# One SBUF port for GpSimd and VectorE in a kernel's scheduler, the float64 shift on ScalarE or VectorE, and longer TensorE fillers

## The chip, the cores and the metric

The kernel runs on one core of one Trainium2 chip. The metric is device time in microseconds (us), the median of several runs of the same program. The engines are named as in the profile: PE is TensorE, PEld its weight loads, DVE is VectorE, ACT is ScalarE, POOL is GpSimd, SP issues the DMAs.

## The reference

Attention (local over a band of seven positions, plus pooled over groups of four) feeds two feed-forward mixtures, all in float32; the weights arrive as float64.

```python
x = attention(q, k, v).transpose(0, 2, 1, 3).reshape(2304, 512)   # 4 batches, 8 heads, 576 x 64
h = x @ w_in                       # 512 -> 2048, float64 weights
x = (h * np.cos(h)) @ w_out        # 2048 -> 512
xn = x / rms * rms_g
g, val = xn @ w_gate, xn @ w_val   # 512 -> 1536
return (silu(g) * val @ w_out2).astype(np.float32)
```

## The kernel before

The program is straight-line code whose order a list scheduler (`Order`, a planner that runs while the program is built) decides. Every stage is a Python generator; before it emits instructions it yields the engine and an assumed duration, or a list of alternatives (engine, duration, release time, activation table, bias). `start` picks the alternative that ends first, bias included; `run` advances the clock of that engine and lets the step of the earliest start and due time go first. So the durations and biases in the `yield` lines set the order of each engine's queue and which engine takes a movable step; on the chip each engine executes its queue in that order, whatever the real durations.

The stages, in the order in which they fill the time:

- Batch 0 of the attention: pooled queries and keys (`sum4`, `pq_ev`, `pooled`), pooled values on POOL (L499 to L506), and five band blocks (`block`): transposes (`btr`, L641), scores (`bs`, L684), softmax on DVE and ACT with a final scaling by the reciprocal sum (L706, on POOL or DVE), a transpose (`bat`, L720) and the product with the values (`bav`, L745). `pooled` scales its exponentials by the reciprocal sum at L555 (POOL or DVE). The sum of both parts is split into a high and a low fp32r half (L768 on ACT, L770 on POOL) and is one tile X.
- Weights. `w_conv` turns a float64 word pair into a high and a low fp32r matrix: a right shift by 29 of the low word (L311, DVE), a `Prelu` that rescales the high word (L315, ACT), a shift-and-or (L317, DVE), a copy to the high half (L319, ACT) and a subtraction for the low half (L322, POOL or DVE; the bias CVB of 9 keeps it on POOL). There are 32 such pieces for the first mixture. `w2_conv` (L1295 to L1299) does the first three steps for 36 pieces of the second mixture. A raw piece occupies one of five places until its last step, and the next weight DMA on SP waits for a place.
- First mixture: 72 units. A unit is `h` on PE (L1004), scaled to integers on ACT (L1022), reduced on DVE (L1024), a sine on ACT (L1027), a product on DVE (L1029), then split into halves `gh` on ACT (L1038) and `gl` on POOL or DVE (L1040, bias GLB), and `y` on PE (L1070). Batches 1 to 3 of the attention run beside it, and exponentials and sines load different activation tables on ACT.
- Second mixture: norms, `gvp` (L1493) and `o` (L1746).

`keep_warm` (L246) puts float32 matmuls into pauses of PE that the planner foresees before its time FT = 90, if a PSUM bank is free: the number is FR = 0.8 of the pause, divided by 0.22.

```python
    n = int((t1 - max(t0, 2.5)) * FR / 0.22)
    have = [x for x in S_.pools["bank"] if x[0] <= t0]
    if t0 > FT or n < 1 or not have:
        return
```

## Time and profile before

| | |
|---|---|
| runs | 984.79 us median (983.96 to 986.35, 3 runs) |
| the profiled execution | 986.51 us, its span 984.7 us |
| PE busy | 954.6 us (97%) |
| DVE, ACT, POOL busy | 724.0, 542.8, 268.5 us |
| mean granted PE clock | 0.994 |

PE is busy nearly all the time, so the view to start from is busy time by stage, then what ended each idle stretch of PE, then the lines of the other engines in the stages where PE is idle. A busy PE can still hold matmuls that do no useful work (the fillers), and in a half-clock stretch it is busy for twice as long.

### The profile page before, as it was taken

The page shows a single profiled execution, that of the slowest core. Times are in us where ns is not written, and L with a number is a line of the kernel's source. Part 1 is how long each engine was busy: PE and PEld are TensorE (multiplying, and loading weights), DVE is VectorE, ACT ScalarE, POOL GpSimd, SP SyncE. Part 2 cuts the span into 40 slices and gives each one's busy share as a digit, 9 for nine tenths or more (in the row PEclk, how much of TensorE's full clock was granted, in tenths as well). Part 3 has the DMA queues.
Part 4 walks back from the last instruction along what each step waited for, and adds up shares of the span by engine and source line. Part 5 has one row for each costly group of instructions (what it writes and reads, how often), then busy time and mean ns, then how long its engine had stood idle before and what let it go on. Part 6 is the DMA issues. An engine that isn't in the chain of part 4 may idle for free.

```text
span 984.7 us, 19115 instructions
## 1 busy us (share of the span) xinstructions
PE 954.6 (97%) x7102; PEld 881.4 (90%) x7102; DVE 724.0 (74%) x1460; ACT 542.8 (55%) x1090; POOL 268.5 (27%) x325
## 2 busy tenths in 40 slices
...
GB/s 245 211 234 252 179 116 118 140 204 185 201 220 153 173 168 137 167 153 165 124 129 65 107 43 49 49 105 93 75 81 70 57 146 131 137 169 137 143 119 76
DMA packets 160333, 136.07 MB, mean 138 GB/s; under 512 B 72176, under 2 KB 133744, under 8 KB 160240
## 3 DMA queue, kind: packets, MB, share of 16 engines
...
q8 instruction: 56, 0.92, 0.4%
q14 instruction: 37, 0.30, 0.1%
HBM read 98.64 MB, written 36.18 MB: 137 GB/s over the span
## 4 chain that ended last, share of the span: by engine, by line
PE 83%; POOL 4%; DVE 3%; SPq 3%; issue 3%; DMA 2%; ACT 2%; DVEq 0%; POOLq 0%; ACTq 0%
PE gvp L1493 26%; PE y L1070 19%; PE h L1004 18%; PE o L1746 13%; PE bav L745 2%; PE btr L641 1%; SPq L475 1%; POOL wwa L322 1%; DMA v<-in_v 1%; SPq L807 1%; PE avp L589 1%; PE bs L684 1%; PE yt L1398 1%; PE bat L720 1%; SPq L478 1%
## 5 line engine op out<-in xcount | busy, mean ns | idle before, releaser
L1493 PE MATMUL gvp<-xc,wc 128*128 128x384 f32 x1296 | 231.7, 335 | 0.0
L1493 PEld LDWEIGHTS gvp<-xc,wc 128*128 128x128 f32 x1296 | 225.6, 188 | 0.3
L1564 DVE TENSOR_TENSOR tmp<-gvp,tmp 128x384 f32<-128x384 f32 x180 | 99.3, 553 | 54.6 <-PE gvp L1493 51.4
L1004 PE MATMUL h<-big,wwa 128*128 128x256 f32 (+1 forms) x756 | 126.1, 320 | 1.6 <-DVE t L1029 1.0
L1004 PEld LDWEIGHTS h<-big,wwa 128*128 128x128 f32 x756 | 109.4, 193 | 11.9 <-DVE t L1029 1.2
L1746 PE MATMUL o<-wo,wc 128*128 128x256 f32 x972 | 118.9, 280 | 0.0
L1746 PEld LDWEIGHTS o<-wo,wc 128*128 128x128 f32 x972 | 116.1, 190 | 0.0
L1070 PE MATMUL y<-wwa,big 128*128 128x512 f32 x432 | 109.6, 398 | 1.7 <-DVE big L1040 1.7
L1070 PEld LDWEIGHTS y<-wwa,big 128*128 128x128 f32 x432 | 78.9, 188 | 18.7 <-DVE big L1040 2.7
L1004 PE MATMUL h<-big,wwb 128*128 128x256 f32 (+1 forms) x504 | 85.2, 320 | 0.1
L1070 PE MATMUL y<-wwb,big 128*128 128x512 f32 x324 | 82.3, 399 | 2.3 <-POOL big L1040 2.3
L1024 DVE SCALAR_TENSOR_TENSOR t<-kk,h 128x512 f32<-128x512 int32 x72 | 49.0, 681 | 42.4 <-ACT kk L1022 42.1
L1004 PEld LDWEIGHTS h<-big,wwb 128*128 128x128 f32 x504 | 73.1, 193 | 7.7 <-issue 0.8
L1022 ACT ACTIVATE kk<-h 128x512 int32<-128x512 f32 x72 | 42.7, 593 | 58.4 <-PE h L1004 58.2
L1070 PEld LDWEIGHTS y<-wwb,big 128*128 128x128 f32 x324 | 59.0, 188 | 14.7 <-POOL big L1040 2.9
L1630 POOL TENSOR_TENSOR wt<-wo 128x256 f32<-128x256 f32 x10 | 9.9, 987 | 208.7 <-DVE wc L1349 183.3
L1029 DVE TENSOR_TENSOR t<-h,t 128x512 f32<-128x512 f32 x72 | 49.3, 685 | 18.1 <-ACT t L1027 17.6
L1555 ACT ACTIVATE tmp<-gvp 128x384 f32<-128x384 f32 x36 | 17.7, 492 | 75.9 <-PE gvp L1493 75.9
L1027 ACT ACTIVATE t<-t,cst 128x512 f32<-128x512 f32 x72 | 51.9, 722 | 13.2 <-DVE t L1024 12.7
L1038 ACT ACTIVATE big<-t 128x512 fp32r<-128x512 f32 x72 | 45.2, 629 | 25.0 <-DVE t L1029 23.6
L1689 ACT ACTIVATE wc<-ut 128x512 fp32r<-128x512 f32 (+1 forms) x60 | 34.3, 584 | 43.4 <-DVE ut L1675 27.2
L1040 DVE TENSOR_TENSOR big<-t,big 128x512 fp32r<-128x512 f32 x54 | 40.0, 741 | 16.5 <-ACT big L1038 16.2
(185 smaller groups left out, 1737.8 us busy)
## 6 DMA issues: line engine op xcount, KB each, us to landing
...
```

What stands on the lines that cost most here:

```text
L1004: PE.matmul(h[:, w_ * ci:w_ * ci + w_], a[:, ksl], x_at(x, kk), start=m == 0, stop=m == 11)
L1022: ACT.activation(out=kk, in_=h, func=ACTF.Copy, scale=INV2PI, bias=0.25)
L1024: DVE.scalar_tensor_tensor(out=t, in0=kk, scalar=TWOPI, in1=h, op0=ALU.mult, op1=ALU.subtract)
L1027: ACT.activation(out=t, in_=t, func=ACTF.Sin, scale=-1.0, bias=cst[:, 0:1])
L1029: DVE.tensor_tensor(out=t, in0=h, in1=t, op=ALU.mult)
L1038: ACT.activation(out=gh, in_=t, func=ACTF.Copy)
L1040: (POOL if e == "POOL" else DVE).tensor_tensor(out=gl, in0=t, in1=gh, op=ALU.subtract)
L1070: PE.matmul(y[j][b], g[:, tsl], a, start=(first and ci == 0 and i == 0), stop=(last and c == 15 and i == 2))
L1493: PE.matmul(bank, w[:, a, kk], xc[:, x, b, kk], start=first and i == 0, stop=i == 5, skip_group_check=True)
L1564: DVE.tensor_tensor(out=half(o), in0=a, in1=half(b), op=ALU.add)
L1689: ACT.activation(out=o[:, 0], in_=src, func=ACTF.Copy)
L1746: PE.matmul(b[m][1][:, l], u[0][x][:, j, l], w[:, y, k], start=(p == 0 and l == 0 and i == 0), stop=(p == C3 - 1 and i == 2), skip_group_c ...
```

## The change

Four things are changed.

1. The planner has a clock for one more resource, `port`. Every POOL step and every DVE step marked "+" needs it and holds it for its duration. Marked are the DVE steps between SBUF operands (shift-and-or, the softmax scalings, the low halves, the norm); those that read PSUM are not.
2. The shift of the low word may go to ACT, by a copy of its upper 16 bits with scale 2^-13 and an offset that makes the conversion to integer truncate.
3. The assumed durations are new, and two biases: CVB from 9 to 0.5, GLB from 0.5 to -0.3. With them the low halves of the weights may go to DVE.
4. Fillers go on up to the planner's time 215: after 90 for pauses of at least 0.8, at 0.6 of the pause, and if no bank is free into the bank that the waiting step is about to write.

```diff
 FT = 90
+FT2, FR2 = 215, 0.6
-CVB, GLB = 9, 0.5
+SHB = 0.0
+CVB, GLB = 0.5, -0.3
...
+            port = eng == "POOL" or eng[-1] == "+"
+            eng = eng.rstrip("+")
...
             t = max(self.free.get(eng, 0.0), t)
+            if port:
+                t = max(self.free.get("port", 0.0), t)
...
+                if port:
+                    self.free["port"] = t + dur
...
-        n = int((t1 - max(t0, 2.5)) * FR / 0.22)
+        own = p.pop("own", None)
+        n = int((t1 - max(t0, 2.5)) * (FR if t0 < FT else FR2) / 0.22)
         have = [x for x in S_.pools["bank"] if x[0] <= t0]
-        if t0 > FT or n < 1 or not have:
+        if n < 1 or t0 > FT2 or t0 > FT and t1 - t0 < 0.8:
             return
-        t = bank_tile(have[0][1], [128, 128], "warm")
+        if have:
+            own = bank_tile(have[0][1], [128, 128], "warm")
+        elif t0 < FT or own is None:
+            return
...
+    def shift(raw, lw):
+        _, e = yield [("DVE+", 0.35), ("ACT", 0.6, None, None, SHB)]
+        if e == "ACT":
+            top = raw.bitcast(U16).rearrange("p (b c) -> p b c", c=4)[:, :, 1]
+            ACT.activation(out=lw, in_=top, func=ACTF.Copy, scale=2.0 ** -13, bias=2.0 ** -14 - 0.5)
+        else:
+            DVE.tensor_scalar(out=lw, in0=lw, scalar1=29, scalar2=None, op0=ALU.logical_shift_right)
...
-        a = yield "DVE", 0.34
-        DVE.tensor_scalar(out=lw, in0=lw, scalar1=29, scalar2=None, op0=ALU.logical_shift_right)
+        yield from shift(raw2, lw)
...
-        _, e = yield [("POOL", 1.5), ("DVE", 0.8, None, None, CVB)]
+        _, e = yield [("POOL", 1.28), ("DVE+", 0.66, None, None, CVB)]
...
-            _, e = yield [("POOL", 0.6), ("DVE", 0.36, None, None, 0.3)]
+            _, e = yield [("POOL", 0.66), ("DVE+", 0.42, None, None, 0.3)]
...
-        _, e = yield [("POOL", 1.3), ("DVE", 0.75, None, None, 0.5)]
+        _, e = yield [("POOL", 1.04), ("DVE+", 0.67, None, None, 0.5)]
...
-        _, e = yield [("POOL", 1.5), ("DVE", 0.8, None, None, GLB)]
+        _, e = yield [("POOL", 1.28), ("DVE+", 0.67, None, None, GLB)]
```

How steps change engines over the whole program, counted in the order of the two programs:

| step | DVE before, now | POOL before, now | ACT before, now |
|---|---|---|---|
| shift of the low word | 68, 16 | | 0, 52 |
| low half of a first-mixture weight | 0, 20 | 32, 12 | |
| scaling in `pooled` (E) | 26, 12 | 6, 20 | |
| scaling in `block` | 15, 4 | 5, 16 | |
| `gl` | 54, 69 | 18, 3 | |
| copy after `bat` | 3, 9 | | 17, 11 |
| activation table loads | | | 43, 49 |

**Place 1, DVE: the first weight pieces and band block 0 of batch 0.** `rawwb` are raw pieces, `bst` and `bE` the block's softmax, `wwa` a converted weight. Before:

```order
L311 TENSOR_SCALAR rawwb_267<-rawwb_267 128x512
L693 TENSOR_REDUCE bst<-bs 128x4
L317 SCALAR_TENSOR_TENSOR rawwb_267<-rawwb_267 128x512
L695 TENSOR_TENSOR bE<-bs,bst 128x4x64
L693 TENSOR_REDUCE bst<-bs 128x4
L311 TENSOR_SCALAR rawwb_281<-rawwb_281 128x512
L695 TENSOR_TENSOR bE<-bs,bst 128x4x64
L317 SCALAR_TENSOR_TENSOR rawwb_281<-rawwb_281 128x512
L701 TENSOR_REDUCE bst<-bE 128x8
L311 TENSOR_SCALAR rawwb_286<-rawwb_286 128x512
L703 TENSOR_SCALAR bst<-bst 128x8
L704 RECIPROCAL bst<-bst 128x8
```

Now, from the shift-and-or of the first piece on:

```order
L337 SCALAR_TENSOR_TENSOR rawwb_267<-rawwb_267 128x512
L722 TENSOR_REDUCE bst<-bE 128x8
L337 SCALAR_TENSOR_TENSOR rawwb_281<-rawwb_281 128x512
L724 TENSOR_SCALAR bst<-bst 128x8
L725 RECIPROCAL bst<-bst 128x8
L342 TENSOR_TENSOR wwa_349<-rawwb_267,wwa_349 128x512
L337 SCALAR_TENSOR_TENSOR rawwb_286<-rawwb_286 128x512
L342 TENSOR_TENSOR wwa_398<-rawwb_281,wwa_398 128x512
L342 TENSOR_TENSOR wwa_439<-rawwb_286,wwa_439 128x512
```

The shifts of the second and third piece have left DVE, and the low halves of the first three pieces have come to it.

**Place 2, POOL: from the pooled values of batch 0 (`v`, `vh`) on.** `E` are the exponentials of `pooled`. Before:

```order
L499 TENSOR_TENSOR v_311<-v_311 128x2x128
L501 TENSOR_TENSOR v_311<-v_311 128x128
L505 TENSOR_TENSOR vh<-v_311 48x2x64
L506 TENSOR_TENSOR vh<-v_311 48x64
```

Now:

```order
L575 TENSOR_TENSOR E<-E,stat 72x6x48
L575 TENSOR_TENSOR E_185<-E_185,stat 72x6x48 x2
L575 TENSOR_TENSOR E_186<-E_186,stat 72x6x48
L575 TENSOR_TENSOR E_187<-E_187,stat 72x6x48 x2
L519 TENSOR_TENSOR v_310<-v_310 128x2x128
L521 TENSOR_TENSOR v_310<-v_310 128x128
```

Six scalings of `E` stand ahead of the value sums. Up to the last value sum of the batch, two low halves of weights (`wwa_349`, `wwa_398`) have left POOL and one scaling of `block` has come.

**Place 3, PE: the first scores of batch 1's `pooled` (`sps`).** `h` and `y` are the mixture's units. Before:

```order
L641 MATMUL btr<-ident,rqk 128x128 x4
L457 MATMUL trq<-ident,qs 64x128
L534 MATMUL sps<-pqs 72x144 x4
L1004 MATMUL h<-big,wwa_522 128x256 x12
L1004 MATMUL h<-big,wwa_682 128x256 x12
```

Now:

```order
L661 MATMUL btr<-ident,rqk 128x128 x4
L1028 MATMUL h<-big,wwa_670 128x256 x12
L554 MATMUL sps<-pqs 72x144 x4
L1028 MATMUL h<-big,wwb_1270 128x256 x12
L1028 MATMUL h<-big,wwb_1323 128x256 x12
L661 MATMUL btr<-ident,rqk 128x128 x4
L259 MATMUL h<-ident 128x128 x6
L1028 MATMUL h<-big,wwa_805 128x256 x12
```

A unit stands between the transposes and the scores, and six fillers (into the bank of the next `h`) stand ahead of a unit. Of the fillers, 108 stand ahead of the first `h` in both programs; in all there are 112 before and 140 now, 24 of the new ones behind the first `y` of the mixture.

## Rows read from the trace of the kernel before

**Rows 1.** Windows: us, busy us of PE, PEld, DVE, ACT, POOL, clock, DMA share, GB/s

```profile
0.00:68.00 68.00, 54.55 (x638) 50.18 (x638) 43.33 (x85) 36.68 (x100) 44.73 (x65) 1.00 0.83 230
68.00:104.00 36.00, 32.81 (x301) 28.83 (x299) 34.36 (x53) 26.85 (x48) 25.75 (x26) 1.00 0.86 248
104.00:126.00 22.00, 19.11 (x137) 15.80 (x138) 20.57 (x41) 19.81 (x41) 14.33 (x18) 0.92 0.62 173
126.00:158.00 32.00, 30.62 (x254) 27.50 (x253) 25.43 (x50) 27.09 (x57) 24.83 (x27) 1.00 0.35 109
158.00:200.00 42.00, 39.19 (x343) 35.45 (x342) 21.44 (x39) 23.03 (x42) 17.57 (x23) 0.92 0.49 138
200.00:380.00 180.00, 178.69 (x1720) 158.88 (x1719) 128.62 (x256) 131.44 (x256) 68.65 (x95) 1.00 0.63 182
380.00:598.00 218.00, 216.63 (x1150) 182.08 (x1148) 150.92 (x311) 132.06 (x252) 46.73 (x49) 1.00 0.35 117
598.00:848.00 250.00, 250.00 (x1442) 249.93 (x1441) 183.63 (x360) 87.68 (x179) 20.41 (x23) 1.00 0.30 89
848.00:985.00 137.00, 132.97 (x1136) 132.76 (x1134) 115.70 (x273) 58.16 (x122) 5.49 (x1) 0.99 0.41 131
```

**Rows 2.** TensorE in order of time: start us, us, what [idle before <-releaser]

```profile
106.16 1.54 PE L534 MATMUL sps<-pqs 64*72 64x144 f32 x8 [2.66 <-DVE bst L704]
138.12 1.43 PE L1070 MATMUL y<-wwb,big 128*128 128x512 f32 x5 [1.09 <-POOL big L1040]
171.25 1.96 PE L745 MATMUL bav<-bt,vb 64*64 64x58 f32 x30 [1.64 <-DVE bt L755]
309.34 2.83 PE L1070 MATMUL y<-wwb,big 128*128 128x512 f32 x11 [1.17 <-POOL big L1040]
```

**Rows 3.** Windows again: the two stretches below full clock

```profile
107.00:110.00 3.00, 3.00 (x17) 2.63 (x15) 3.00 (x7) 2.97 (x4) 1.75 (x3) 0.56 0.83 237
171.00:178.00 7.00, 6.75 (x53) 6.62 (x54) 2.80 (x5) 2.00 (x5) 5.83 (x8) 0.51 0.52 110
```

**Rows 4.** VectorE by line and shape: count | busy us, mean ns | idle before

```profile
L311 DVE TENSOR_SCALAR rawwa<-rawwa 128x512 int32<-128x512 int32 x18 | 12.0, 673 | 6.2 <-DMA rawwa<-in_moe_w_out 6.2
L311 DVE TENSOR_SCALAR rawwb<-rawwb 128x512 int32<-128x512 int32 x14 | 9.8, 713 | 0.0
L555 DVE TENSOR_TENSOR E<-E,stat 72x288 f32<-72x288 f32 x26 | 14.2, 572 | 0.8
L706 DVE TENSOR_TENSOR bt<-bt,bst 128x512 f32<-128x512 f32 x11 | 9.7, 884 | 0.2
L1040 DVE TENSOR_TENSOR big<-t,big 128x512 fp32r<-128x512 f32 x54 | 40.0, 741 | 16.5 <-ACT big L1038 16.2
```

**Rows 5.** Source view of line L703: minimum/median/maximum ns, first and last start

```profile
L703 DVE TENSOR_SCALAR bst<-bst x20: 136/172/1259, 36.2 to 425.6; 128x8 f32<-128x8 f32 x20
```

**Rows 6.** GpSimd by line and shape, columns as in Rows 4

```profile
L1040 POOL TENSOR_TENSOR big<-t,big 128x512 fp32r<-128x512 f32 x18 | 24.5, 1359 | 99.6 <-ACT big L1038 97.0 <-issue 2.5
L322 POOL TENSOR_TENSOR wwa<-rawwb,wwa 128x512 fp32r<-128x512 f32 x10 | 14.0, 1409 | 4.0 <-ACT wwa L319 3.9
L555 POOL TENSOR_TENSOR E<-E,stat 72x288 f32<-72x288 f32 x6 | 6.3, 1057 | 20.1 <-DVE stat L551 8.2 <-ACT big L1038 5.3 <-ACT kk L1022 4.0
L706 POOL TENSOR_TENSOR bt<-bt,bst 128x512 f32<-128x512 f32 x4 | 4.5, 1113 | 26.0 <-ACT big L768 13.4 <-DVE bst L704 12.6
```

**Rows 7.** GpSimd in order of time, as in Rows 2

```profile
27.12 0.73 POOL L499 TENSOR_TENSOR v<-v 128x256 f32<-128x256 f32 x1 [5.20 <-DMA v<-in_v]
45.16 4.08 POOL L322 TENSOR_TENSOR wwa<-rawwb,wwa 128x512 fp32r<-128x512 f32 x3
```

**Rows 8.** ScalarE by line and shape, columns as in Rows 4

```profile
L1027 ACT ACT_TABLE_LOAD x21 | 26.9, 1283 | 0.4
```

**Rows 9.** ScalarE in order of time, as in Rows 2: two `Prelu` in a row

```profile
104.24 1.24 ACT L315 ACTIVATE rawwa<-rawwa 128x512 f32<-128x512 f32 x2
```

**Rows 10.** A filler run on TensorE in order of time

```profile
47.10 2.27 PE L246 MATMUL warm<-ident 128*128 128x128 f32 x18
```

More of the change, by code (lines that the diff above doesn't have):

```diff
@@ L12 @@
 I32 = mybir.dt.int32
+U16 = mybir.dt.uint16
 ACTF = mybir.ActivationFunctionType
@@ L154, in start @@
             if best is None or t + dur + bias < best[0]:
-                best = (t + dur + bias, t, eng, dur, tab, sw)
+                best = (t + dur + bias, t, eng, dur, tab, sw, port)
         return best[1], best[1:]
@@ L177, in run @@
             else:
-                t, eng, dur, tab, sw = step
+                t, eng, dur, tab, sw, port = step
                 if sw and TP is not None:
@@ L183, in run @@
                 if eng == "PE" and self.fill:
-                    self.fill(self.free.get(eng, 0.0), t)
+                    self.fill(self.free.get(eng, 0.0), t, p)
                 self.free[eng] = t + dur
+                if port:
+                    self.free["port"] = t + dur
                 p["t"], p["eng"] = t + dur, eng
@@ L236, in fused_kernel, with keep_warm @@
     ACT.activation(out=ident_r, in_=ident, func=ACTF.Copy)
-    def keep_warm(t0, t1):
-        n = int((t1 - max(t0, 2.5)) * FR / 0.22)
+    def keep_warm(t0, t1, p):
+        own = p.pop("own", None)
+        n = int((t1 - max(t0, 2.5)) * (FR if t0 < FT else FR2) / 0.22)
         have = [x for x in S_.pools["bank"] if x[0] <= t0]
-        if t0 > FT or n < 1 or not have:
+        if n < 1 or t0 > FT2 or t0 > FT and t1 - t0 < 0.8:
             return
-        t = bank_tile(have[0][1], [128, 128], "warm")
+        if have:
+            own = bank_tile(have[0][1], [128, 128], "warm")
+        elif t0 < FT or own is None:
+            return
         for _ in range(n):
-            PE.matmul(t, ident, ident, start=True, stop=True)
+            PE.matmul(own, ident, ident[:, :own.shape[-1]], start=True, stop=True, skip_group_check=True)
     S_.fill = keep_warm if FR else None
@@ L305, in w_conv @@
         w = p[1] if p[2] == "wg" else p[0].tile([128, 2, 512], F32R, tag=p[1], name="w" + p[1])
+        raw2 = raw
         raw = raw.rearrange("p (b c) -> p b c", c=2)
@@ L309, in w_conv @@
         yield "ACT", 0.0
-        a = yield "DVE", 0.34
-        DVE.tensor_scalar(out=lw, in0=lw, scalar1=29, scalar2=None, op0=ALU.logical_shift_right)
+        yield from shift(raw2, lw)
         yield "ACT", 0.62
         ACT.activation(out=c, in_=c, func=ACTF.Prelu, scale=2.0 ** -112, alpha=-2.0 ** 32)
-        yield "DVE", 0.7
+        yield "DVE+", 0.66
         DVE.scalar_tensor_tensor(out=hw, in0=hw, scalar=3, in1=lw, op0=ALU.logical_shift_left, op1=ALU.bitwise_or)
@@ L347, in x_tiles @@
                     ACT.activation(out=X[t][0][:, k:k + 2], in_=x[:, k:k + 2], func=ACTF.Copy)
-                    _, e = yield [("POOL", 1.5), ("DVE", 0.7, None, None, 0.5)]
+                    _, e = yield [("POOL", 1.28), ("DVE+", 0.66, None, None, 0.5)]
                     (POOL if e == "POOL" else DVE).tensor_tensor(out=X[t][1][:, k:k + 2], in0=x[:, k:k + 2], in1=X[t][0][:, k:k + 2], op=ALU.subtract)
@@ L548, in pooled @@
         done(("exp", b, hp))
-        yield "DVE", 0.16
+        yield "DVE+", 0.33
         DVE.tensor_scalar(out=sm, in0=sm, scalar1=1e-9, scalar2=4.0, op0=ALU.add, op1=ALU.mult)
@@ L674, in block @@
             held.append((i, bank_tile(i, [128, 4, 64], "bs")))
+        S_.cur["own"] = held[0][1][:, 0:2].rearrange("p a k -> p (a k)")
         yield "PE", 1.0
@@ L738, in block @@
             held.append((i, bank_tile(i, [128, 4, 116], "bav")))
+        S_.cur["own"] = held[0][1][:, 0]
         yield "PE", 1.0
@@ L768, in block @@
                 ACT.activation(out=xh, in_=bx[:, :, at:at + l], func=ACTF.Copy)
-                yield "POOL", 0.1 + 0.011 * l
+                yield "POOL", 0.15 + 0.0088 * l
                 POOL.tensor_tensor(out=xl, in0=bx[:, :, at:at + l], in1=xh, op=ALU.subtract)
@@ L998, in unit @@
             wh, wl = W[1, 2 * c]
+            if ci == 0:
+                S_.cur["own"] = h[:, 0:128]
             yield "PE", 1.44 if len(cs) > 1 else 2.76
@@ L1293, in w2_conv @@
         yield "ACT", 0.0
-        yield "DVE", 0.34
-        DVE.tensor_scalar(out=lw, in0=lw, scalar1=29, scalar2=None, op0=ALU.logical_shift_right)
+        yield from shift(raw, lw)
         yield "ACT", 0.62
         ACT.activation(out=f, in_=f, func=ACTF.Prelu, scale=2.0 ** -112, alpha=-2.0 ** 32)
-        yield "DVE", 0.7
+        yield "DVE+", 0.66
         DVE.scalar_tensor_tensor(out=raw[:, 0:512], in0=hw, scalar=3, in1=lw, op0=ALU.logical_shift_left, op1=ALU.bitwise_or)
@@ L1310, in lo_on @@
     def lo_on(m, both):
-        dve = ("DVE", 0.15 + m / 960, None, None, 0.3)
-        return [("POOL", 0.1 + m / 330), dve] if both else [dve]
+        dve = ("DVE+", 0.14 + m / 960, None, None, 0.3)
+        return [("POOL", 0.17 + m / 450), dve] if both else [dve]
     def splits():
@@ L1375, in norm @@
         ss, m, q, z = (st[:, 2 * x:2 * x + 2] for x in range(4))
-        yield "DVE", 1.9
+        yield "DVE+", 1.9
         DVE.tensor_scalar(out=m, in0=ss, scalar1=1.0 / DM, scalar2=1e-6, op0=ALU.mult, op1=ALU.add)
@@ L1413, in n_scale @@
     def n_scale(t, y, q, h):
-        _, e = yield [("ACT", 0.62, (S_.cur["t"], "DVE")), ("DVE", 0.45, (S_.cur["t"], "DVE"))]
+        _, e = yield [("ACT", 0.62, (S_.cur["t"], "DVE")), ("DVE+", 0.46, (S_.cur["t"], "DVE"))]
         if e == "ACT":
```

4 lines of the change are left out of this document (2 added, 2 removed).

## The prediction

> **What bounds the kernel now.** I read the windows by stage first, because a share over the whole span hides where PE waits. From 598 to 848 us PE is busy 250.00 of 250 us, and its weight loads 249.93 [rows 1]: nothing that DVE, ACT or POOL does there can be worth time unless it makes PE wait. From 200 to 598 PE is idle 1.3 + 1.4 us, in the tail 4.0 us. What can be won lies ahead of 200 us. There PE is idle 13.5 us up to 68, and 3.2, 2.9, 1.4 and 2.8 us in the four stages from 68 to 200, 10.3 us together [rows 1]. In these four stages DVE is the fullest engine first (34.4 of 36 us, then 20.6 of 22), then ACT (19.8 of 22, 27.1 of 32).
>
> Next I read what ended PE's waits, in order of time. The three longest behind 80 us are 2.66 us for a DVE softmax step, 1.64 us for a DVE sum behind `bav`, and 1.09 us for a `gl` on POOL; one more `gl` on POOL costs 1.17 us at 309 [rows 2]. Two of them are followed by half clock: granted 0.56 over 3 us and 0.51 over 7 us [rows 3]. The level there is 1.2 instead of 2.4 GHz, and PE loses 0.44 x 3 + 0.49 x 7 = 4.7 us of full-speed work.
>
> Why is DVE full? The source view of L703 shows it: an operation on 128x8 elements takes 0.17 us in the median and 1.26 us at worst [rows 5]. Work of that size does not vary by itself; it was held up, by about as long as POOL's larger operations take (1.06 to 1.41 us [rows 6]). The shift takes 0.67 to 0.71 us on average [rows 4], the planner assumed 0.34. So the order before was made for a DVE that is faster than the real one when POOL works.
>
> **The change, part by part.** The sum is made against the profiled execution, 986.5 us with a span of 984.7; the median of the runs is 984.8, 1.7 lower, and I carry the difference over to it.
>
> A. Up to the first `h` (68 us). POOL's pooled values start at 27.12 us after 5.20 us of waiting for their DMA [rows 7]. Six scalings of E now stand ahead of them (place 2): 6 x 1.06 = 6.3 us [rows 6], of which between none and 5.2 us fits into that wait. Ahead of the last value sum two low halves go (2 x 1.41 = 2.8) and a scaling comes (1.1) [rows 6]. So the value sums end between 6.3 - 5.2 - 2.8 + 1.1 = -0.6 and +4.6 us later; what is late then is the first `bav`. Against it: the low halves of the first three pieces, the last of which sat in a run of 4.08 us on POOL that began at 45.16 [rows 7], are on DVE behind fewer shifts (place 1), so that the raw places come free earlier, and SP now has the loads of band blocks 2 to 4 ahead of those of the next pooled queries, and PE 29 instead of 36 fillers between the first `bav` and the first `h`: 7 x 0.25 = 1.8 us (18 records, two for each filler, in 2.27 us [rows 10]). The number of fillers ahead of the first `h` is 108 in both programs, so the planner still foresees the same pauses. I take 0, ends -4 and +4.6; the lower end is the 4.08 us run.
>
> B. From 68 to 200 us. Counted in the order up to the product (L1029) of unit 3, DVE loses 20 shifts (20 x 0.70 = 14.0 us), 6 scalings of E (3.4) and 4 of `block` (3.5), and gains 10 low halves. These have no row on DVE; the nearest is `gl`, the same shape and types, at 0.74, the dearest like it the `block` scaling at 0.88 [rows 4]. I take 0.74: 7.4 us. DVE is relieved by 13.5 us (12.1 at the other end) in and ahead of the two stages in which it is full. That removes the 2.66 us wait; of the 1.64 us wait, which lies behind them, I count half; the 1.09 us goes because `gl` goes from 54 to 69 of 72 on DVE. Together -4.6. Of the 4.7 us lost to half clock, the part behind the first wait goes (1.3) and half of the other (1.7): -3.0.
>
> What comes in return. First, ACT gets the shifts: 25 of 32 in the first mixture. No row shows a shift on ACT; the nearest is the `Prelu` on the same strided tile, two in 1.24 us [rows 9], so 0.62 each. Ends: 0.31, as it reads two bytes of each word instead of four, and 1.24, if such reads are as slow as two of the other. I take 0.62, the row of the same shape. Counted in the order up to `gh` of unit 12, ACT has 25 shifts more (15.5 us), 4 table loads more (4 x 1.28 = 5.1 [rows 8]) and 11 other steps less (6.8 at the same 0.62): +13.8 us. By unit 3 it is 18 shifts, one load less and 10 other steps less: +3.7, and the stage from 68 to 104 has 9.1 us free. The other 10.1 fall into the stages from 104 on, which have 2.2, 4.9 and 19.0 us free [rows 1]. So all of it can hide; if it has to be done by 158, 3.0 us reach PE, and at the dear end of the shift (7 more x 0.62) 7.3. I take +1.3. Second, 24 fillers of 0.25 us = 6.0 us stand behind the first `y`. In a pause that exists they cost nothing; in one that doesn't, all matmuls behind them wait. I take a quarter, +1.5; ends 0 and 6.0. B is -4.6 - 3.0 + 1.3 + 1.5 = -4.8; ends -15.0 (all idle time and clock loss) and +10.
>
> C. Behind 200 us. The `gl` wait at 309 goes: -1.2. The shifts of the second mixture (27 of 36 on ACT) and the other steps that change engines lie beside a PE that is 99% busy: 0.
>
> Sum: 0 - 4.8 - 1.2 = **-6.0 us**, 980.5 for an execution like the profiled one, and 984.8 - 6.0 = **978.8 us** for the median.
>
> **A rule against the row.** A table load takes 1.283 us, and the 21 of the sine line have 0.4 us of idle time ahead of them in all [rows 8]. The order has six more of them. The Trainium skill (ScalarE: Activation LUTs, section "What ACT_TABLE_LOAD costs") says that a switch also drains the engine for about 1.38 us, 2.66 us in all. No such drain shows in the rows of this trace. By that rule the four more loads ahead of unit 12 would cost ACT an estimated 5.5 us more than I count, and the time would be some 984.
>
> **The rivals.**
> - *The order drifts.* The port exists in the planner alone; on the chip the queues run freely, so DVE and POOL collide as before, at other places. For it: POOL's and DVE's queues have waits on PE and DMA that the planner guesses. Against it: 20 low halves and 15 `gl` leave POOL, 35 x 1.4 = 49 us, and 25 scalings come, 27 us, so there is less to collide with. Only the two `gl` waits (2.3 us) go and fillers cost 1.5: 984.0. This is also the case in which the port does not do what it says.
> - *ACT takes DVE's place.* From 104 to 158 ACT is the engine with the least room. It decides when more than the free 7.1 us are asked for there; then sines and exponentials come late, and `y` and `tra` with them. Price 7.3 (above), with half of the fillers unwanted (3.0), against the waits that go (4.6) and C (1.2); the clock loss stays: 984.8 + 7.3 + 3.0 - 5.8 = 989.3, slower. For it: 27.1 of 32 us busy already; against it: ACT takes no part in the port, and the planner assumes 0.6 for a step that takes 0.62.
> - *The drain.* By the rule above, as a mechanism here: each switch stalls ACT once more for as long as the load. The 0.4 us in 21 loads speaks against it [rows 8]. The 5.1 us of loads ahead of unit 12 would count twice: 984.
> - *All waits go.* With real durations nothing unforeseen is left: B at -12 of its -15, A at -1: 984.8 - 14.2 = 970.6.
>
> **How the numbers follow.** My forecast, 975 to 981.8, gets 0.41; all waits gone 0.17; the drift 0.19; the drain 0.03; ACT 0.20. A measurement of this kernel can tell 0.3%, 3 us, from no change (981.8 to 987.7). So faster is 0.58, same 0.22, slower 0.20. The range reaches to the slow rival's value (990) and past the fast one by most of A's lower end (968), and leaves out some 0.13. The forecast's own range is 975 to 981.8.
>
> **What would show it.** Right: DVE from 68 to 126 busy well under 95%; no PE wait over 2 us between 90 and 200 us; granted clock 1.00 in all stages from 68 on; PE's idle time from 68 to 200 near 5 us; no `gl` on POOL ahead of a `y` wait; first `h` within 4 us of 67.8. Wrong: PE waits for ACT lines (L1051, L565) from 104 to 160, ACT busy over 95% there; the 128x8 scaling still at over 1 us; half clock behind fillers that did not suffice; or the first `bav` 3 us late and the first `h` with it.

## The result, and the profile after

The changed kernel takes 996.16 us (median of 6 runs, 994.22 to 1000.68), the kernel before in the same rounds 985.19 us (983.96 to 986.35): a ratio of 1.0115 [1.0099, 1.013]. It is slower by 11 us. The profiled execution took 997.53 us, its span is 995.5 us.

The windows by stage after, in the columns of [rows 1]:

```profile
0.00:68.00 68.00, 50.88 (x560) 46.96 (x560) 39.29 (x75) 38.91 (x103) 39.93 (x66) 0.96 0.83 227
68.00:104.00 36.00, 34.89 (x370) 32.51 (x371) 24.26 (x41) 31.00 (x56) 20.37 (x23) 0.93 0.79 220
104.00:126.00 22.00, 19.73 (x156) 16.86 (x155) 19.04 (x35) 21.03 (x37) 11.36 (x14) 1.00 0.67 195
126.00:158.00 32.00, 31.64 (x244) 27.74 (x243) 24.81 (x52) 30.69 (x62) 17.92 (x21) 1.00 0.35 95
158.00:200.00 42.00, 41.27 (x367) 37.38 (x367) 21.13 (x37) 26.98 (x55) 14.45 (x22) 1.00 0.49 145
200.00:380.00 180.00, 175.42 (x1642) 154.64 (x1640) 119.46 (x238) 142.58 (x271) 65.88 (x103) 0.99 0.63 177
380.00:598.00 218.00, 215.85 (x1202) 178.63 (x1202) 141.06 (x298) 128.58 (x242) 30.45 (x30) 1.00 0.37 119
598.00:848.00 250.00, 248.20 (x1433) 247.29 (x1432) 182.10 (x372) 88.56 (x183) 21.63 (x24) 1.00 0.29 86
848.00:985.00 137.00, 137.00 (x1146) 136.77 (x1145) 124.63 (x288) 65.47 (x136) 3.91 (x4) 1.00 0.45 140
```

From 68 to 200 us TensorE is idle for 1.1 + 2.3 + 0.4 + 0.7 = 4.5 us instead of 10.3, and DVE has room (24.3 of 36 us instead of 34.4). But up to 68 us TensorE is idle for 17.1 us instead of 13.5, its clock is 0.93 in the stage behind, and from 200 to 848 it is idle for 8.5 us instead of 2.7.

TensorE in order of time after, the four longest waits behind 60 us and the first `h`, in the columns of [rows 2]:

```profile
68.32 1.96 PE L767 MATMUL bav<-bt,vb 64*64 64x58 f32 x32 [4.60 <-ACT bt L748]
...
75.50 3.12 PE L1028 MATMUL h<-big,wwa 128*128 128x256 f32 x24
...
106.74 1.43 PE L1094 MATMUL y<-wwa,big 128*128 128x512 f32 x5 [1.18 <-DVE big L1064]
...
334.99 1.00 PE L609 MATMUL avp<-at,vh 128*128 128x144 f32 x6 [2.44 <-DVE at L599]
...
608.26 1.09 PE L1421 MATMUL yt<-ident,y 128*128 128x128 f32 x8 [1.31 <-ACT y L1439]
```

None of the four waits of [rows 2] is left at its length. A wait of 4.60 us stands ahead of a `bav`, and the first `h` follows at 75.50 us, 7.7 us later than before; the next large one, 2.44 us, lies at 335 us.

Both of these lead to ScalarE. Its queue in order of time from 60 us (columns as in [rows 9]; `L317` is the shift):

```profile
60.10 0.63 ACT L720 ACTIVATE bE<-bE 128x512 f32<-128x512 f32 x1 [1.41 <-DVE bE L716]
64.60 0.67 ACT L317 ACTIVATE rawwb<-rawwb 128x512 int32<-128x512 uint16 x1 [3.87 <-DMA rawwb<-in_moe_w_in]
65.17 0.64 ACT L339 ACTIVATE wwa<-rawwb 128x512 fp32r<-128x512 f32 x1
65.72 0.65 ACT L335 ACTIVATE rawwb<-rawwb 128x512 f32<-128x512 f32 x1
66.27 0.65 ACT L339 ACTIVATE wwa<-rawwb 128x512 fp32r<-128x512 f32 x1
66.83 0.82 ACT L416 ACTIVATE pqs<-trq 64x256 f32<-64x256 f32 x2
67.67 0.60 ACT L748 ACTIVATE bt<-bat 128x512 f32<-128x512 f32 x1
```

The `bat` that the copy L748 reads had been done since 62.6 us. The copy ran at 67.67 us, because six steps stand ahead of it (the last five lines before it; L416 is two), the first of which waited 3.87 us for a weight's DMA. SyncE's own queue shows when that DMA was issued:

```profile
54.41 3.98 SPq L829 DMA_DIRECT2D vb<-in_v  x5
...
60.19 0.39 SPq L299 DMA_DIRECT2D rawwb<-in_moe_w_in  x1
```

It left at 60.19 us, behind loads of `vb` and pooled queries, and landed 4.4 us later. At 329 us the same thing happens, now with a piece of the second mixture, whose products start at 570 us; `bat`, `gh` (L1062) and the attention's copy `at` (L597) stand behind it:

```profile
329.66 0.68 ACT L317 ACTIVATE rawwa<-rawwa 128x512 int32<-128x512 uint16 x1 [3.10 <-DMA rawwa<-in_moe_w_out]
330.25 0.58 ACT L748 ACTIVATE bt<-bat 128x512 f32<-128x512 f32 x1
...
331.20 1.15 ACT L1062 ACTIVATE big<-t 128x512 fp32r<-128x512 f32 x2
...
334.20 0.39 ACT L597 ACTIVATE at<-tra 128x288 f32<-128x288 f32 x1
```

VectorE shows who waits for that: its `gl` (L1064) for 3.31 us of `gh`, and then its part of `at` (L599) for 1.21 us of ScalarE's. TensorE's `avp` waits for this last one.

```profile
331.87 1.55 DVE L1064 TENSOR_TENSOR big<-t,big 128x512 fp32r<-128x512 f32 x2 [3.31 <-ACT big L1062]
334.62 0.31 DVE L599 COPY at<-tra 128x144 f32<-128x144 f32 x1 [1.21 <-ACT at L597]
```

Over the whole program the shifts on ScalarE wait 19.2 us for DMA, in 14 places (source view of L317: minimum/median/maximum ns; then what ended its idle time, us and times):

```profile
L317 ACT ACTIVATE rawwa<-rawwa x40: 656/675/701, 85.8 to 437.6; 128x512 int32<-128x512 uint16 x40
...
L317 ACT ACTIVATE rawwb<-rawwb x12: 656/680/713, 29.8 to 85.2; 128x512 int32<-128x512 uint16 x12
...
  DMA rawwa<-in_moe_w_out: 7.1, 6
  DMA rawwa<-in_moe_w_val: 5.4, 3
  DMA rawwb<-in_moe_w_in: 3.9, 1
  DMA rawwa<-in_moe_w_gate: 2.8, 4
```

And these two stops are each followed by a stretch of half clock, 0.50 of full speed from 68 to 72 us and a mean of 0.91 over 20 us from 320 on (windows):

```profile
68.00:72.00 4.00, 3.68 (x41) 3.57 (x42) 2.50 (x5) 2.50 (x5) 0.00 (x0) 0.50 0.14 39
320.00:340.00 20.00, 16.93 (x160) 14.14 (x158) 11.81 (x23) 16.17 (x33) 12.48 (x19) 0.91 0.63 163
```

**Where the 10.8 us lie.** For every kernel below I reckoned a position from its one profiled execution: each matmul counts with the median time from its start to the next matmul's start that its kind has in the trace of before, the fillers count nothing, and I compare the times at which two kernels have done the same sum. Against the kernel before, the changed one is 6.1 us behind at 70 us, level at 200, 0.2 ahead at 300, 6.2 behind at 350, 9.7 at 570, 10.8 at 650 and 10.4 at 975. At 583 us of before the two have done exactly the same matmuls, so the 9.7 there depends on no weights; at 200 they have not, and other weights move that figure by up to 3 us. So up to 200 us a gain like the one that I forecast pays for the early stop, and the loss is made behind 300 us, where I had counted 0.

### The profile page after: what moved, and what is told of

It reads as the page before. It is cut to its first block, busy times and chain, and to the rows that moved or that the text cites. A ratio compares the mean times of both kernels' runs of the same rounds, so it can differ in the third digit from the quotient of the medians.

```text
span 995.5 us, 19180 instructions
## 1 busy us (share of the span) xinstructions
PE 961.3 (97%) x7158; PEld 885.0 (89%) x7158; DVE 698.3 (70%) x1436; ACT 574.2 (58%) x1140; POOL 225.9 (23%) x305
## 4 chain that ended last, share of the span: by engine, by line
PE 77%; DMA 7%; SPq 5%; ACT 4%; DVE 4%; issue 2%; POOL 1%; DVEq 0%; ACTq 0%; POOLq 0%
PE gvp L1516 26%; PE y L1094 17%; PE h L1028 15%; PE o L1769 13%; DMA wfs<-rawwa 2%; SPq L813 2%; DMA rawwa<-in_moe_w_val 1%; PE bav L767 1%; DMA rawwa<-in_moe_w_out 1%; PE avp L609 1%; PE btr L661 1%; SPq L495 1%; SPq L829 1%; DMA rqk<-in_q 1%; PE yt L1421 1%
## 5 line engine op out<-in xcount | busy, mean ns | idle before, releaser
L1028 PEld LDWEIGHTS h<-big,wwa 128*128 128x128 f32 x756 | 107.2, 190 | 12.0 <-DVE bt L672 1.2
L1028 PE MATMUL h<-big,wwb 128*128 128x256 f32 (+1 forms) x504 | 82.5, 316 | 0.0
L1064 DVE TENSOR_TENSOR big<-t,big 128x512 fp32r<-128x512 f32 x69 | 50.1, 728 | 17.1 <-ACT big L1062 16.5
L1053 DVE TENSOR_TENSOR t<-h,t 128x512 f32<-128x512 f32 x72 | 49.3, 686 | 18.0 <-ACT t L1051 17.7
L1712 ACT ACTIVATE wc<-ut 128x512 fp32r<-128x512 f32 (+1 forms) x60 | 34.4, 586 | 45.5 <-DVE ut L1698 28.3
L1051 ACT ACTIVATE t<-t,cst 128x512 f32<-128x512 f32 x72 | 51.7, 721 | 12.0 <-DVE t L1048 11.1
L1062 ACT ACTIVATE big<-t 128x512 fp32r<-128x512 f32 x72 | 44.9, 625 | 13.7 <-DVE t L1053 12.6
```

The costliest lines, as they stand in the source:

```text
L1028: PE.matmul(h[:, w_ * ci:w_ * ci + w_], a[:, ksl], x_at(x, kk), start=m == 0, stop=m == 11)
L1051: ACT.activation(out=t, in_=t, func=ACTF.Sin, scale=-1.0, bias=cst[:, 0:1])
L1053: DVE.tensor_tensor(out=t, in0=h, in1=t, op=ALU.mult)
L1062: ACT.activation(out=gh, in_=t, func=ACTF.Copy)
L1064: (POOL if e == "POOL" else DVE).tensor_tensor(out=gl, in0=t, in1=gh, op=ALU.subtract)
L1712: ACT.activation(out=o[:, 0], in_=src, func=ACTF.Copy)
```

## The experiments

Theories. **Q**: a shift on ScalarE that meets a DMA not yet landed stands at the head of ScalarE's queue and delays what is behind it. **D**: the new order on DVE and POOL costs. **F**: the added fillers cost. Later **W** (the work of the shifts on ScalarE), **C** (a chance of the order: every edit of a step's time gives the planner another order), **N** (the norm) and **Q2** (below) join them. "before" is run beside each, 984.3 to 985.1 us.

**1. One wait, all other queues unchanged.** ScalarE's two first steps of the ninth piece are held until the bat copy is issued.

```diff
+    def later(f, n):
+        on_act.extend([0] * n)
+        held_act.append(f) if held_act and not n or n and len(on_act) in HOLD else f()
...
-            ACT.activation(out=ba, in_=t, func=ACTF.Copy)
+            ACT.activation(out=ba, in_=t, func=ACTF.Copy); b or release()
```

> The changed kernel (996.2 us) with one difference: on ScalarE the shift and the Prelu of the ninth weight piece stand behind the copy after bat of band block 2 instead of ahead of it; every other queue is as it was. Theory Q (a shift on ScalarE waits for its piece's DMA at the head of ScalarE's queue, and what stands behind it is late): the wait of 4.60 us ahead of that block's bav goes, the first h starts at 69 to 71.5 us instead of 75.5, and the time is 990 to 992.5. Rival D (what costs time is the new order on DVE and POOL that the port clock makes): another wait takes the place at once, first h later than 73, time 995 to 997. Rival F (the added fillers cost): no change, 995 to 997.

994.29 us (990.47 to 997.3, 4 runs); repeated below. ScalarE and TensorE there:

```profile
62.19 0.83 ACT L416 ACTIVATE pqs<-trq 64x256 f32<-64x256 f32 x2
63.05 0.60 ACT L748 ACTIVATE bt<-bat 128x512 f32<-128x512 f32 x1
63.54 0.66 ACT L317 ACTIVATE rawwb<-rawwb 128x512 int32<-128x512 uint16 x1
...
66.36 0.67 ACT L317 ACTIVATE rawwb<-rawwb 128x512 int32<-128x512 uint16 x1 [1.01 <-DMA rawwb<-in_moe_w_in]
```

```profile
63.70 1.14 PE L767 MATMUL bav<-bt,vb 64*64 64x58 f32 x32 [0.85 <-ACT bt L748]
...
68.11 1.14 PE L767 MATMUL bav<-bt,vb 64*64 64x58 f32 x32 [1.80 <-ACT bt L748]
...
70.48 3.11 PE L1028 MATMUL h<-big,wwa 128*128 128x256 f32 x24
```

The bat copy runs at 63.05 instead of 67.67 us, the 4.60 us wait is 0.85 us, the first `h` comes at 70.48 instead of 75.50, as Q said. The median lies above Q's 990 to 992.5. A smaller wait of the same kind is left: another shift meets its DMA (1.01 us), the next block's copy stands behind it, and that block's `bav` waits 1.80 us. At 200 us this execution is 4.7 us ahead of before; it then loses 7.4 up to 570.

**2. Seven more shifts of the second mixture, each just ahead of its own `Prelu`.** The list of held shifts goes from one to eight.

> As the kernel before it, and seven more shifts on ScalarE (of the second mixture's weights, those that waited most) stand just ahead of their own Prelu. Theory Q: the avp wait of 2.44 us at 335, the gh waits near 304 and 323 and the half clock behind them go too, 4 to 6 us more: 985 to 988. Rival D: no more than 1 us less than the kernel before it. Rival F: 995 to 997.

991.83 us (990.87 to 997.32, 4 runs): Q's 985 to 988 is missed, and the runs cover the same stretch as those of 1. The wait at 335 us is gone, but a held shift still waits 2.37 us for DMA at 340, ScalarE stands for 2.75 us ahead of another shift at 352, and an `avp` waits 2.19 us for `at` on ScalarE at 358. From 200 to 570 us it still loses 7.8.

**3. Without the added fillers.** `FT2` from 215 to 90.

> The changed kernel without the fillers behind the planner's time 90; the order of everything else is the same. Rival F: the fillers stand in pauses that are not there, 24 of them at 0.25 us, so 989.5 to 992. Theory Q: most of them stand in real pauses, 994.5 to 997; and 997 to 1000 if the clock falls to its lower level without them.

997.61 us (996.89 to 1001.89, 4 runs). F falls: the fillers cost nothing that these runs show. The clock does fall without them, two of the windows in the columns of [rows 1]:

```profile
104.00:126.00 22.00, 20.73 (x153) 17.97 (x154) 17.62 (x32) 19.51 (x38) 12.01 (x15) 0.92 0.66 172
126.00:158.00 32.00, 29.52 (x204) 25.11 (x202) 24.34 (x49) 29.45 (x57) 16.11 (x19) 0.89 0.31 89
```

**4. All shifts on VectorE.**

```diff
-        _, e = yield [("DVE+", 0.35), ("ACT", 0.6, None, None, SHB)]
+        _, e = yield "DVE+", 0.35
```

> The changed kernel with every shift on VectorE: port clock, new durations and fillers stay, and the planner makes its order anew. Theory Q: no wait for a weight's DMA on ScalarE but those of the Prelu, first h at 66 to 71, time 980 to 988. Rival D: first h later than 73, time 993 to 998. Rival F: 993 to 998.

986.14 us (981.94 to 990.69, 10 runs), ratio to before 1.0021 [1.0003, 1.0038]. With the shifts on VectorE, in an order made anew, ten of the eleven microseconds are gone, and the first `h` comes at 69.6 us. D falls as the main cause. Whether it is the wait, the work on ScalarE or the other order, this run does not tell.

**5. The wait of 1 moved, and the second mixture's shifts on VectorE.** Theory Q2: ScalarE's shifts pay up to 200 us and cost behind it.

```diff
-        yield from shift(raw, lw)
+        yield from shift(raw, lw, False)
```

> The kernel in which the ninth piece's two ScalarE steps stand behind the bat copy (994.3 us, its profiled execution 990.5, which is 6 us ahead of the kernel before at 300 us and loses 8 us behind it), and all shifts of the second mixture's weights on VectorE; those of the first mixture as planned, on ScalarE or VectorE. Theory Q2 (ScalarE's shifts pay up to 200 us, where VectorE is full, and cost behind it, where they wait for DMA ahead of gh, the bat copies and the sines, and VectorE has room): the lead of 5 to 6 us at 300 stays until 570, ScalarE's waits for the second mixture's DMA go, 979 to 983. Rival D (the order that the port clock makes costs behind 300 us wherever the shift runs): the lead is lost as before, 988 to 993.

991.05 us (986.7 to 995.74, 8 runs): Q2 is missed and D's range hit. The lead is 3.7 us at 200 and gone at 275. VectorE and TensorE there:

```profile
244.81 0.43 DVE L319 TENSOR_SCALAR rawwa<-rawwa 128x512 int32<-128x512 int32 x1 [4.11 <-DMA rawwa<-in_moe_w_gate]
245.15 0.68 DVE L722 TENSOR_REDUCE bst<-bt 128x8 f32<-128x512 f32 x1
...
246.87 0.68 DVE L1053 TENSOR_TENSOR t<-h,t 128x512 f32<-128x512 f32 x1
```

```profile
247.60 1.84 PE L1028 MATMUL h<-big,wwa 128*128 128x256 f32 x12 [3.01 <-DVE t L1053]
```

The same thing on the other engine: the shift waits 4.11 us for its DMA at the head of VectorE's queue, the softmax and the product (L1053) stand behind it, and TensorE waits 3.01 us for the product. Behind 200 us VectorE's shifts wait 19.0 us in all. So VectorE is no safe place either; before, its shifts waited 5.4 us there, and no wait of TensorE over 1.2 us followed. Against D as the reason speaks run 4, which has the port clock and all shifts on VectorE and loses nothing from 200 to 570 us.

**6. The norm without the port mark.**

```diff
-        yield "DVE+", 1.9
+        yield "DVE", 1.9
```

> As the kernel before it, and the norm's step of 1.9 us is not marked as a user of the port. Theory N (the port mark makes the norm wait in the plan for four GpSimd sums, in the trace it starts 4.3 us behind the last square instead of at once, and yt is late by 1.3 to 1.8 us): 1 to 2 us less than the kernel before it, no yt wait over 1 us near 600. Rival: VectorE's small steps collide with GpSimd there and take back what is won: within 0.5 us of the kernel before it.

991.07 us (985.74 to 998.13, 10 runs). N falls and its rival holds: the norm starts at once, but its small steps then take 0.65 to 1.14 us beside POOL, and `yt` waits 2.75 us.

**7. Before, with the shift on ScalarE or VectorE and nothing else.**

```diff
-        a = yield "DVE", 0.34
-        DVE.tensor_scalar(out=lw, in0=lw, scalar1=29, scalar2=None, op0=ALU.logical_shift_right)
+        yield from shift(raw2, lw)
```

> The kernel before with one difference: its planner may put the shift on ScalarE (VectorE 0.34, ScalarE 0.6, no bias). No port, old durations, old fillers. Theory Q2: a gain of 3 to 5 us where VectorE is full (68 to 200 us), and waits of ScalarE for the weights' DMA of 10 to 20 us in all, which reach TensorE behind 200 us: 984 to 992. Rival D: the shift on ScalarE is a pure gain, 978 to 982.

992.49 us (988.68 to 994.48, 4 runs), a little above Q2's range: the shift's alternative, in the order that it makes, costs 7 us without port, new durations or fillers. This execution is 3.3 us ahead of before at 200 us and loses 11.1 from there to 570, as Q2 says. Its row by line and shape, in the columns of [rows 4]:

```profile
L305 ACT ACTIVATE rawwa<-rawwa 128x512 int32<-128x512 uint16 x29 | 19.5, 674 | 18.2 <-DMA rawwa<-in_moe_w_val 9.4 <-DMA rawwa<-in_moe_w_gate 5.6 <-DMA rawwa<-in_moe_w_out 2.7
```

**8. ScalarE's alternative released later.** In the plan ScalarE may have the shift only AL = 4.0 us behind the landing that the planner assumes.

```diff
-        _, e = yield [("DVE+", 0.35), ("ACT", 0.6, None, None, SHB)]
+        t0 = S_.cur["t"] + AL
+        _, e = yield [("DVE+", 0.35), ("ACT", 0.6, (t0, S_.cur["eng"]), None, SHB)]
```

> The changed kernel with one rule more: ScalarE's alternative for the shift is released in the plan 4.0 us behind the landing that the planner assumes, VectorE's at the landing. Theory Q: most shifts go to VectorE or stand on ScalarE behind their DMA; ScalarE's waits for weights' DMA fall from 19 us to under 6; 983 to 989. Rival D: 993 to 998.

977.05 us (974.93 to 978.36, 4 runs), ratio to before 0.991 [0.989, 0.9931]: **faster than both kernels**, and faster than Q's range. 14 shifts are left on ScalarE and none of them waits; the windows from 68 us show most of the idle time and the half clock gone (fillers count as busy):

```profile
L319 ACT ACTIVATE rawwa<-rawwa 128x512 int32<-128x512 uint16 x10 | 6.7, 670 | 0.0
...
L319 ACT ACTIVATE rawwb<-rawwb 128x512 int32<-128x512 uint16 x4 | 2.7, 678 | 0.0
```

```profile
68.00:104.00 36.00, 35.48 (x323) 32.41 (x319) 29.66 (x53) 33.15 (x59) 22.29 (x25) 1.00 0.81 220
104.00:126.00 22.00, 22.00 (x214) 19.79 (x213) 21.08 (x39) 18.79 (x37) 13.99 (x18) 1.00 0.81 217
126.00:158.00 32.00, 30.85 (x209) 26.28 (x207) 26.25 (x47) 28.54 (x61) 16.28 (x20) 1.00 0.46 130
```

**9 and 10. The same with 2.0 and 7.0 us.**

> The kernel with the late release of ScalarE's alternative (977.1 us at 4.0 us, 14 shifts on ScalarE), with 2.0 instead of 4.0 us: 15 shifts go to ScalarE. Theory Q (what counts is whether a shift on ScalarE meets a DMA that has not landed): waits of ScalarE's shifts for DMA of 0 to 5 us, time 977 to 984, rising with these waits. Rival C (each reorder of the plan falls by chance, and 977 was a lucky one): anything from 977 to 993, with no link to these waits.

983.25 us (980.96 to 984.07, 10 runs); the shifts on ScalarE wait 3.6 us for DMA.

> The same with 7.0 us: 8 shifts on ScalarE, all behind their DMA. Theory Q: no waits of these shifts for DMA, VectorE somewhat fuller from 68 to 126 us, 977 to 983. Rival C: anything from 977 to 993.

985.01 us (983.39 to 986.83, 10 runs), with no such waits, outside Q's range. So the waits do not order these three: the position at 200 us does (5.8, 1.2 and, at 4.0 us, 10.4 us ahead). Part of the 977 is the order that this number happens to give (C).

**11. The kernel of 8 without the added fillers.**

> The kernel with 4.0 us, without the fillers behind the planner's time 90; the rest of the order is the same. By the run without them of the changed kernel (1.5 us longer, within its spread): 976 to 980. If they stand in no real pause, 24 at 0.25 us: 971 to 974.

978.5 us (977.77 to 980.84, 4 runs). As in 3, the fillers are worth 0 to 1.5 us.

**12. All shifts on VectorE, and no port clock.**

```diff
-            port = eng == "POOL" or eng[-1] == "+"
+            port = False
```

> The kernel with all shifts on VectorE (986.1 us) and without the port clock: a POOL step and a marked VectorE step may overlap in the plan again; durations, biases and fillers stay the changed ones. If the port clock is worth something: VectorE's 128x8 steps at 1 us and more again, TensorE waits for VectorE's softmax, 988 to 994. Rival: the clock gives nothing, since the queues run freely, 983 to 987.

991.98 us (987.06 to 993.54, 5 runs), 6 us above run 4: `bat` waits 3.32 and 3.38 us for VectorE's scaling of `block` at 67 and 85 us. Whether the missing port clock or the chance of another order (C) makes these 6 us is open: a 128x8 scaling of over 1 us stands in both (1.06 here, 1.26 in run 4).

**13 and 14. The kernel of 8 in its order, 32 shifts moved from VectorE to ScalarE.** First at the same place of the program, then just ahead of their own `Prelu`: wait, work and order apart (`False` in the place of `True` issues it at its place).

```diff
-        if e == "ACT":
+        if e == "ACT" or hold is not None:
...
+            hold.append(f) if hold is not None and True else f()
```

> The kernel with the late release of 4.0 us (977.1 us), every queue in its order, with one difference: the 32 shifts of the second mixture's weights that stand on VectorE are issued on ScalarE, each at the same place of the program. Theory Q (a shift on ScalarE that meets a DMA not yet landed makes the bat copies, gh and sines behind it late): ScalarE's shifts wait 10 to 20 us for DMA in all, TensorE gets new waits between 200 and 450 us, 981 to 988. Rival C (the earlier difference was the chance of another order): the order is the same, so 976 to 979. Rival W (it is the work on ScalarE, 32 at 0.67 us, not the wait): slower too, 980 to 985, and the next kernel as slow.

979.78 us (978.51 to 983.37, 6 runs).

> The same 32 shifts on ScalarE, and all 36 of the second mixture just ahead of their own Prelu, which is on ScalarE in every version: the same work on ScalarE, but no wait for DMA that the Prelu did not have, or nearly none. Theory Q: no more than 2 us above 977 (the shift delays the Prelu by 0.67 us each): 976 to 979. Rival W: as slow as the kernel with the 32 shifts at their place, 980 to 985. Rival C: 976 to 979 as well.

978.83 us (977.01 to 981.45, 6 runs). The rows of the shift, by line and shape:

```profile
L316 ACT ACTIVATE rawwa<-rawwa 128x512 int32<-128x512 uint16 x42 | 27.9, 668 | 7.0 <-DMA rawwa<-in_moe_w_gate 3.5 <-DMA rawwa<-in_moe_w_val 2.2 <-DMA rawwa<-in_moe_w_out 1.3
```

```profile
L316 ACT ACTIVATE rawwa<-rawwa 128x512 int32<-128x512 uint16 x42 | 28.1, 669 | 3.6 <-DMA rawwa<-in_moe_w_gate 2.7 <-DMA rawwa<-in_moe_w_val 0.8
```

The first has 3.4 us more of wait and is 1 us slower, which the spread of the runs covers. Against run 8, which ran in other rounds, they are 2.7 and 1.8 us slower by their medians. In run 13 every range is missed, W's by a little; in run 14 W's is missed, Q's and C's hold. The waits are 7.0 us instead of Q's 10 to 20, less than half of the changed kernel's 19.2, so this pair does not try the cause at its size.

**15 and 16. Run 1 again, beside the changed kernel.**

> The kernel with the ninth piece's two ScalarE steps behind the bat copy, timed again in more rounds beside the changed kernel itself, since its four runs (990.5, 991.4, 997.2, 997.3) lie apart. Theory Q: 3 to 6 us below the changed kernel of the same rounds. Rival D: within 1.5 us of it.

994.76 us (993.88 to 997.16, 4 runs); the wait is 0.63 us (2.57 us ahead of the next block's `bav`), the first `h` at 72.60.

> The changed kernel itself, for the comparison with the one before it: 994 to 998 by its own earlier runs, in every theory.

998.44 us (993.8 to 1001.07, 6 runs); the wait is 5.17 us, the first `h` at 75.25. So the early wait is worth 3.7 us between these medians, 1.9 between the first ones, with single runs that overlap; by position at 200 us it is some 5 us: 3.2, 4.7 and 5.2 ahead (this edit, and run 2, which holds it) against 0.0 and 2.5 behind.

**17 and 18. The late release on both engines, in two plans without common ground.**

```diff
-        _, e = yield [("DVE+", 0.35), ("ACT", 0.6, (t0, S_.cur["eng"]), None, SHB)]
+        _, e = yield [("DVE+", 0.35, (t0, S_.cur["eng"])), ("ACT", 0.6, (t0, S_.cur["eng"]), None, SHB)]
```

> The changed kernel, with the shift released 4.0 us behind the landing that the planner assumes on both engines, not on ScalarE alone: 27 shifts on ScalarE instead of 52 (or of 14 with the release on ScalarE alone, 977.1 us). Theory Q (a shift that meets its DMA at the head of an engine's queue delays what stands behind it, on VectorE as on ScalarE): waits of shifts for DMA under 3 us on both engines together, 974 to 981. Rival C (the order falls by chance): 977 to 993. Rival W (work on ScalarE): 13 shifts more there than with 14, so 978 to 983.

992.46 us (990.47 to 994.46, 6 runs).

> The kernel before with the shift on ScalarE or VectorE (992.5 us, ScalarE's shifts wait 18 us for DMA), and the shift released 4.0 us later on both engines; 20 shifts on ScalarE; no port, old durations. Theory Q: waits of shifts for DMA under 4 us, and 978 to 986, so the sign of the same idea turns with the release alone. Rival C: 980 to 995.

994.3 us (991.51 to 997.16, 6 runs). Q's times are missed in both, though the waits did go (1.3 and 1.8 us on the two engines, then 0 and 2.0). Behind 200 us the first runs as Q says, 2.0 us gained up to 570; the second loses 2.4. Both are behind already at 200, by 9.5 and 2.9 us. In the first, the first `h` comes at 73.8 us, and at 142 us TensorE waits 2.72 us for a product on VectorE, after which the clock is 0.89 over the stage from 126 to 158 us.

**All of them by position** (us behind the kernel before, minus is ahead, in one profiled execution each; waits for DMA ahead of shifts on the two engines, behind 200 us):

| kernel | median | up to 200 | 200 to 570 | 570 to 975 | waits ScalarE, VectorE |
|---|---|---|---|---|---|
| changed | 996.2 | 0.0 | +9.7 | +0.7 | 14.5, 14.0 |
| 16 changed again | 998.4 | +2.5 | +10.9 | +0.6 | 14.9, 14.9 |
| 3 no new fillers | 997.6 | +2.9 | +7.7 | +0.7 | 15.2, 15.7 |
| 1 one wait | 994.3 | -4.7 | +7.4 | +0.7 | 12.2, 13.7 |
| 15 one wait again | 994.8 | -3.2 | +10.3 | +0.9 | 12.5, 14.4 |
| 2 eight shifts | 991.8 | -5.2 | +7.8 | +1.2 | 9.5, 15.2 |
| 7 before + ScalarE | 992.5 | -3.3 | +11.1 | +0.1 | 16.7, 8.9 |
| 5 second mixture on VectorE | 991.1 | -3.7 | +7.2 | +0.9 | 0, 19.0 |
| 6 norm unmarked | 991.1 | -2.7 | +3.2 | +2.8 | 0, 14.8 |
| 13 at place | 979.8 | -10.2 | +3.3 | +1.1 | 5.6, 0 |
| 14 at `Prelu` | 978.8 | -9.9 | +2.2 | +0.7 | 3.0, 0 |
| 9 release 2.0 | 983.3 | -5.8 | +2.3 | +1.1 | 2.7, 8.5 |
| 8 release 4.0 | 977.1 | -10.4 | +1.3 | +0.9 | 0, 4.9 |
| 11 and no new fillers | 978.5 | -10.8 | +2.3 | +0.7 | 0, 6.7 |
| 10 release 7.0 | 985.0 | -1.2 | 0.0 | +0.6 | 0, 10.6 |
| 4 all on VectorE | 986.1 | -0.9 | -0.9 | +1.0 | 0, 9.1 |
| 12 and no port | 992.0 | +3.0 | +3.7 | -0.9 | 0, 11.4 |
| 17 both late | 992.5 | +9.5 | -2.0 | -0.9 | 0, 1.7 |
| 18 before, both late | 994.3 | +2.9 | +2.4 | -0.2 | 0, 2.0 |

## Why the prediction was wrong

The forecast was 978.8 us, range 968 to 990; measured were 996.2.

**Part B, "-4.8", came out in size; which of its parts made it is another matter.** From 68 to 200 us the changed kernel gains 5.9 us by position, and 2.9 in run 16; with the early wait taken away it stands 3.2 to 5.2 us ahead of before at 200 us (runs 1, 2 and 15). Several of the signs came: DVE at 24.3 of 36 us from 68 to 104, no wait over 1.18 us between 90 and 200 us, 4.5 us of idle time ("near 5"), no `gl` on POOL ahead of a `y` wait there. "Granted clock 1.00 in all stages from 68 on" held from 104 to 200 us alone, and of the signs of being wrong one came: ACT is busy over 95% from 104 to 158, though TensorE does not wait for it over 0.6 us there.

Two of the good signs, the idle time and the clock, are in good part the fillers' doing: without the added ones, in the same order (run 3), TensorE is idle 8.0 us from 68 to 200, the clock falls to 0.89, and that execution gains 0.7 us there. And by these single executions the gain goes with the shift on ScalarE rather than with the port clock: run 7, without port clock, new durations or added fillers, gains 5.7 us from 68 to 200, run 4, which has all three and no shift on ScalarE, none (0.2 lost).

Two things in my sum do not hold: before, `y` also waits 1.17 us at 96.4 us for a `gl` on VectorE, longer than the 1.09 us that I called the third wait, and such a wait is still there (1.18 us at 106.7); and the end of +10 does not follow from its terms, which give 7.3 + 6.0 = 13.3 with nothing won.

The worst 128x8 scaling takes 421 instead of 1259 ns [rows 5], by the source view of that line:

```profile
L724 DVE TENSOR_SCALAR bst<-bst x20: 157/172/421, 35.3 to 431.7; 128x8 f32<-128x8 f32 x20
```

In runs 4 and 8 it is 1.26 and 1.25 us again. Of the 20 such steps, 4 to 7 take over 0.4 us in the four kernels without the port clock (before and runs 7, 12, 18), 0 to 3 in those with it: such meetings become rarer, they are not excluded. The 1.5 us that I charged for fillers are not there (runs 3 and 11). ScalarE is fuller than I said, 21.0 of 22 and 30.7 of 32 us from 104 to 158. The shift takes 0.67 us, I took 0.62.

**Part A, "I take 0, ends -4 and +4.6", failed.** The first `h` is 7.7 us late, outside my ends. What I weighed there happened and was not what made it late: POOL's values are late and the first `bav` comes at 48.88 instead of 46.02 us, but the second comes 2.9 us earlier. The stop came from the step that I had moved without its wait: I costed the shift on ScalarE as 0.62 us of work, and did not ask what its DMA does, or what is queued behind it on ScalarE. Run 1 changes that one thing: the stop of 4.60 us goes, and 1.80 us come back one block later behind the next shift's DMA.

**Part C, "The shifts of the second mixture ... lie beside a PE that is 99% busy: 0", failed, by some 10 us.** From 200 to 570 us the changed kernel loses 9.7 us, although the 1.17 us wait for a `gl` at 309 is gone as I said. A TensorE that was 99% busy came to wait 2.44 us for one late input, and I gave the shifts no wait. Seven kernels whose shifts wait 9 us or more for DMA on ScalarE behind 200 us lose 7.4 to 11.1 us from 200 to 570; run 5, where VectorE waits 19.0 us in its place, loses 7.2, and the other eleven lose at most 3.7. Six of the seven share one plan, so run 7 is the only independent one. That a waiting shift stops TensorE was seen in the chains at 329 us and, on VectorE, at 244 us. That these waits make the whole loss is not shown: run 2, which takes some 3 us of them away and leaves all other queues as they are, loses as much as run 1, and in runs 13 and 14, where the waits are small, the 32 shifts cost 2 to 3 us against another round's run. How much of the 9.7 us is wait, how much work on ScalarE and how much the order stays open.

**Behind 570 us** 0.6 to 1.2 us more are lost in nearly all kernels with the port clock (2.8 in run 6, 0.9 won in run 17), -0.9 to 0.1 us in the three others without it. In the changed kernel that is the place of the `yt` wait at 608 us. Run 6 speaks against the norm's mark as the reason. It stays open.

**The rivals.** "ACT takes DVE's place", 989.3 us with a chance of 0.20, named the engine and the sign, but for work in a stage that had room, not for a wait. The Trainium skill's strict order of the ScalarE, VectorE and GpSimd queues (PSUM — Partial Sum Buffer, section "Engine vs sequencer instructions") is the rule I should have weighed; the trace agrees, with a copy whose input had been done for 5 us standing behind a waiting shift. The drain at table loads can be struck out, 24 loads of the sine line have 0.4 us of idle time ahead of them:

```profile
L1051 ACT ACT_TABLE_LOAD x24 | 30.8, 1283 | 0.4
```

"The order drifts" was right in a way that I had not priced: the same rule with another number (2.0, 4.0, 7.0 us) gives 983, 977 and 985 us, and releasing the shift late on both engines gives 992. A change of the planner's numbers carries several us of its own, and my forecast's own range of 975 to 981.8 left no room for that.
